# Loading raw second-layer weights into the home of their low part, in a fused attention and two-layer-pair kernel

## The chip, the cores and the metric

The kernel runs on one core of a Trainium2 chip. The metric is the device time of one execution in microseconds, as the median of several runs.

## The reference

Causal attention with a decay term feeds a first pair of dense layers (a softmax-gated activation and a layer norm between them) and then a second pair (squared ReLU between them). What matters here is the last part:

```python
def _moe2_ref(x, w_in, w_out):          # x 2304 x 512, w_in 512 x 2048, w_out 2048 x 512
    h = np.maximum(x @ w_in, 0.0)
    return (h * h @ w_out).astype(np.float32)
...
attn_out = _attn_ref(**attn_kwargs)
x = np.ascontiguousarray(attn_out.transpose(0, 2, 1, 3)).reshape(B * S, H * D)
x = _moe_ref(x=x, **moe_kwargs)
return _moe2_ref(x=x, **moe2_kwargs)
```

All arrays are float32.

## The kernel before

**Precision.** TensorE multiplies numbers in the rounded format fp32r. Each float32 operand is therefore split into a high part (its rounding, made by a copy) and a low part (the operand less its high part, made by a subtraction on VectorE), and each product is three: high x low, low x high, high x high. Line 1139, `halves`, emits the two operations: the rounding by `copy` (line 376 on ScalarE, line 380 on GpSimd, line 382 on VectorE), the subtraction on line 1144.

**Stages.** Attention runs tile by tile, and the first layer pair follows it token block by token block (lines 860 to 862 for its first layer, 811 to 813 for its second). Under both, the second pair's weights are read from the inputs, put together from words of 64-bit numbers, combined for a Strassen scheme and stored to DRAM as w2d, w2u, w2f and w2s; five staging buffers in the tile free serve for that. Then comes the second pair. The first 256 tokens go up in a plain form (`half_up`, line 1334, eight pairs p of feature blocks, products written into z). The other 2048 go up in 32 units of seven Strassen products (`unit`, line 1386). Each pair of each block goes down in a step of seven products (`step`, lines 1487 to 1489, 21 matmuls).

**Weights and homes.** The up weights of the plain form come from w2d, 16 loads of 512 columns (`weightsh`, line 1173). The down weights of seven of the eight pairs come from w2f in four loads each, "a" of 256 columns and "b", "s", "t" of 512 (`weights2`, line 1192); the eighth pair has its split parts stored in w2s and loads them direct (line 1212). Each high or low part lives in a home carved from a tile that an earlier stage used: the attention's k tiles, its pt, the first pair's weights wih, wil, woh, wol, the staging tile free, e and others. `claim` (line 1003) adds a step with no work to the plan that makes a home wait for its last use by the earlier stage.

**The raw ring.** A raw weight is loaded by `load2` (line 1157, transfer on line 1164) into the next of six raw buffers: kn0, kn1, vn4, vn5, x and adj1 (`RAW`, line 1049). `halves` then rounds it from there into the high home and subtracts into the low home; when the subtraction is done, the raw buffer is free. The token blocks of the units use the same six: `xload` (transfer on line 1224), `xdiff` (line 1241), `xsplit` (`halves` into homes in wol, q2 and vn).

**Order.** No engine's order is written by hand. Each operation is a step of a plan, with its engines and costs, a priority (a due time) and what it reads and writes. `lay` (line 127) simulates the five engines with these costs and takes, for each engine, the ready step that starts first, or within a slack the most urgent. A step that falls ready earlier can so pass others on every engine. Raw loads have the priority of their use less AHEAD = 10000 ns; claims had that of the use itself. All transfers are issued by SyncE, one after the other; each holds its waits there.

Of the kernel before, what the change touches and what calls it, by code (L numbers as in the profile page):

```python
# [8 lines left out]
F32 = mybir.dt.float32  # L9
# [4 lines left out]
ALU = mybir.AluOpType  # L14
# [13 lines left out]
class Plan:  # L28
# [11 lines left out]
        dve=dict(pe=230, dve=127, act=198, pool=203, dma=1230),  # L40
        act=dict(pe=110, dve=142, act=153, pool=160, dma=1234),
        pool=dict(pe=135, dve=75, act=75, pool=88, dma=1200),
        dma=dict(pe=1500, dve=1450, act=1410, pool=1450, dma=1790),
# [225 lines left out]
def tile_kernel(ctx: ExitStack, tc: tile.TileContext, q, k, v, f, w_in, w_out, g_ln, w2_in, w2_out, out):  # L269
    nc = tc.nc  # L270
# [31 lines left out]
    w2d = dram.tile([KF2, P, 512], F32, name="w2d")  # L302
    w2u = dram.tile([KF2 // 2, 7, P, 512], F32, name="w2u")
    w2f = dram.tile([KF2 // 2 - NPRE, 7, P, 256], F32, name="w2f")
# [55 lines left out]
    pl = Plan(dict(pp=3, hp=2, rq=NRQ), ("z0", "z1", "xo", "h", "h0", "h1"))  # L360
# [9 lines left out]
    def copy(n, dst, src, prio, reads, writes, uses=(), scale=None, psum=True):  # L370

        def fn():
            x = 1.0 if scale is None else scale
            if s.on == "act":
                if scale is None:
                    nc.scalar.copy(dst(), src())  # L376
                else:
                    nc.scalar.activation(out=dst(), in_=src(), func=AF.Copy, scale=scale)
            elif s.on == "pool":
                nc.gpsimd.tensor_scalar(out=dst(), in0=src(), scalar1=x, scalar2=1.0, op0=ALU.mult, op1=ALU.mult)  # L380
            elif scale is None:
                nc.vector.tensor_copy(dst(), src())
            else:
                nc.vector.tensor_scalar(out=dst(), in0=src(), scalar1=scale, scalar2=None, op0=ALU.mult)

        ap = not (scale is None or isinstance(scale, float))
        ns = dict(act=(51 if psum else 94) + 0.833 * n + (93 if ap else 0))
        ns["dve"] = 67 + 1.042 * n if psum else 68 + 0.522 * n + (61 if ap else 0)
        if not psum:
            ns["pool"] = (244 if ap else 161) + 0.833 * n  # L390
        s = pl.add(ns, fn, prio, reads, writes, uses=uses, port=not psum)
        return s
# [596 lines left out]
    def carve(tag, sizes, dt=F32R, old=None):  # L989

        memo = {}
        out, o = [], 0
        for n in sizes:
            def get(o=o, n=n):
                if "t" not in memo:
                    memo["t"] = new(tag, [sum(sizes)], dt)
                return memo["t"][:, o : o + n]

            out.append((get, held[tag] if old is None else old))
            o += n  # L1000
        return out

    def claim(piece, keys, prio):

        if piece[1]:
            pl.add(dict(dve=0), lambda: None, prio, [], list(piece[1]) + list(keys))

    def rk2(ri):
        return [("2r", ri, z) for z in range(2)]
# [10 lines left out]
    c = carve("woh", [512] * 7 + [256] * 2)  # L1020
# [8 lines left out]
    c = carve("q2", [512] * 4)  # L1029
# [17 lines left out]
    HU = upper[:6] + large[at_h:]  # L1047
    SX2 = carve("adj1", [640], F32, rk2(5))[0]
    RAW = [carve(a, [512], F32)[0] for a in ("kn0", "kn1", "vn4", "vn5", "x", "adj1")]
# [89 lines left out]
    def halves(raw, rk, hi, hk, lo, lk, n, prio, uses=()):  # L1139

        copy(n, hi, raw, prio, rk, [hk], uses, None, False)

        def sub():
            nc.vector.tensor_tensor(out=lo(), in0=raw(), in1=hi().bitcast(F32), op=ALU.subtract)  # L1144

        pl.add(dict(dve=67 + 1.045 * n), sub, prio, list(rk) + [hk], [lk], uses=uses, port=True)
# [3 lines left out]
    def once(nm, piece, keys, prio):  # L1150
        if nm not in first_use:
            first_use.add(nm)
            claim(piece, keys, prio)

    turn = [0]

    def load2(src, rk, n, prio):
        ri = turn[0] % len(RAW)
        turn[0] += 1
        once(("raw", ri), RAW[ri], rk2(ri), prio)  # L1160

        def fn():
            dst = RAW[ri][0]()[:, 0:n]
            nc.sync.dma_start(dst.rearrange("p (c x) -> p c x", x=256) if len(src.shape) == 3 else dst, src)

        pl.add(dict(dma=LOAD2 * n / 512), fn, prio - AHEAD, rk, rk2(ri)[0 : n // 256])
        return ri

    W2 = {p: {} for p in range(KP)}
    H2 = {p: {} for p in range(KP)}  # L1170
    hkeys = {}

    def weightsh(p, prio):
        for c in range(2):
            ri = load2(w2d[2 * p + c], [("w2d", 2 * p + c, z) for z in range(2)], 512, prio)
            for a in "hl":
                m = 4 * p + 2 * c + "hl".index(a)
                hkeys[m] = ("w2", p, f"u{c}{a}")
                H2[p][f"u{c}{a}"] = HU[m]
                claim(HU[m], [hkeys[m]], prio)  # L1180
            W = H2[p]
            halves(
                RAW[ri][0], rk2(ri), W[f"u{c}h"][0], ("w2", p, f"u{c}h"), W[f"u{c}l"][0], ("w2", p, f"u{c}l"), 512, prio
            )

    def again(piece):
        for m, x in enumerate(HU):
            if x is piece:
                return (piece[0], [hkeys[m]])
        return piece  # L1190

    def weights2(p, prio):
        W = W2[p]
        o = 0
        for nm, n in (("a", 256), ("b", 512), ("s", 512), ("t", 512)):
            c = range(o, o + n // 256)
            o += n // 256
            for a in "hl":
                W[nm + a] = again((small if n == 256 else large).pop(0))
                claim(W[nm + a], [("w2", p, nm + a)], prio)  # L1200
            if p < KP - NPRE:
                src = w2f[p, c[0]] if n == 256 else w2f[p, c[0] : c[0] + 2].rearrange("c p x -> p c x")
                ri = load2(src, [("w2f", p, k) for k in c], n, prio)
                halves(
                    lambda ri=ri, n=n: RAW[ri][0]()[:, 0:n], rk2(ri)[0 : n // 256], W[nm + "h"][0], ("w2", p, nm + "h"),
                    W[nm + "l"][0], ("w2", p, nm + "l"), n, prio,
                )
                continue
            for y, a in enumerate("hl"):
                def fn(dst=W[nm + a][0], c=c, n=n, y=y):  # L1210
                    src = w2s[p + NPRE - KP, c[0] : c[0] + n // 256, :, y * 256 : y * 256 + 256]
                    nc.sync.dma_start(
                        dst().bitcast(F32).rearrange("p (c x) -> p c x", x=256), src.rearrange("c p x -> p c x")
                    )

                pl.add(
                    dict(dma=LOAD2 * n / 512), fn, prio - AHEAD, [("w2s", p, k) for k in c], [("w2", p, nm + a)]
                )

    def xload(ri, g, tok, prio):  # L1220
        once(("raw", ri), RAW[ri], rk2(ri), prio)

        def fn():
            nc.sync.dma_start(
                RAW[ri][0]().rearrange("p (c x) -> p c x", x=TB), x2d[:, 2 * g : 2 * g + 2, tok : tok + TB]
            )

        rk = [("x2d", cc, tok // P + t) for t in range(TPB) for cc in (2 * g, 2 * g + 1)]
        pl.add(dict(dma=1140), fn, prio - 2000, rk, rk2(ri))

    def xsplit(ri, j, prio):
        for a in range(2):
            once(("xo", j, a), XOP[j][a], [("xo", j, a)], prio)
        halves(RAW[ri][0], rk2(ri), XOP[j][0][0], ("xo", j, 0), XOP[j][1][0], ("xo", j, 1), 512, prio)
# [10 lines left out]
    def x_half(prio):  # L1245
        for g in range(2):
            xload(g, g, 0, prio)
            xsplit(g, 5 + g, prio)
        turn[0] = 2

    def x_block(b, prio):
        tok = TB + 2 * TB * (b - 1)
# [306 lines left out]
    for y, (a, e) in enumerate(((0, P), (P, S))):  # L1559
        w = slice(a, e)  # L1560
        n = e - a

        def scan(w=w, a=a):
# [8 lines left out]
                out=fl[:, w], in0=fl[:, w], scalar1=1e-4, scalar2=1.0, op0=ALU.max, op1=ALU.min  # L1572
# [91 lines left out]
    t0 = TEND + P2  # L1664
    t1 = t0 + KP * 2800
    x_half(t0 - W2X)
    for x in ORDER:
        nm, p = x[0], int(x[1])
        if nm == "u":
            weightsh(p, t0 - W2H + 2800 * p)  # L1670
        elif nm == "d":
            weights2(p, t1 - W2D + 4830 * p)
        elif nm == "h":
            half_up(p, t0 + 2800 * p)
        else:
            x_block(1, t1 - 9000)
    todo = [(0, p) for p in range(KP)]
    done = 0
    for b in range(1, NTB // 2 + 1):
        for p in range(KP):  # L1680
            n = (b - 1) * KP + p
# [27 lines left out]
AHEAD = 10000.0  # L1709
# [18 lines left out]
NPRE, LOAD2 = 1, 900  # L1728
# [54 lines left out]
```

## Time and profile before

| | |
|---|---|
| runs | 830.59, 824.18 and 828.28 us, median 828.28 |
| the profiled execution | 824.09 us |
| its span in the profile | 822.3 us |
| TensorE busy, mean granted clock | 800.7 us, 0.997 |
| stages, as the trace shows them | attention and first pair to about 468 us; plain up products (L1334) 447 to 483; units and steps from 479 |

Times in the trace count from the start of the span. A row of a timeline gives the start, the duration, the engine, the line, the output and inputs by tile name with numbers left out, and in brackets the idle time before it with what ended it. Matmuls overlap, so a run of n products lasts about n pitches and one tail. "Granted clock" is the share of TensorE's full speed of 2.4 GHz that it was given.

### The profile page before, as it was taken

How to read it: one execution, taken by the hardware profiler on the slowest of the kernel's cores; microseconds unless marked ns; L12 is line 12 of the kernel's file. 1: busy time of each engine (PE TensorE's matmuls, PEld its weight loads, DVE VectorE, ACT ScalarE, POOL GpSimd, SP SyncE). 2: the span in 40 equal slices, each digit the busy share in tenths (PEclk: the TensorE clock that was granted, in tenths of full speed). 3: DMA queues.
4: the chain of work that ended last, by engine and by line, in shares of the span. 5: the costliest groups of instructions: out<-in, count | busy, mean ns of one | idle time of the engine just before them, and what ended most of it. 6: DMA issues, size and time to landing. Idle time of an engine off the chain costs nothing.

```text
span 822.3 us, 19212 instructions
## 1 busy us (share of the span) xinstructions
PE 800.7 (97%) x6648; PEld 734.4 (89%) x6648; DVE 635.1 (77%) x1624; ACT 547.8 (67%) x1409; POOL 390.8 (48%) x539
## 2 busy tenths in 40 slices
PE   8899999999999999999999998999999999999997
PEld 7687777888888888888989998999999999999997
DVE  8898777878886667686658779779778867987776
ACT  6899988888797779899777676445335343533332
POOL 6467776767768777687777411021111121112110
PEclk9999999999999999999999999999999999999999
DMA  6643346657665554765557889896867767665401
GB/s 206 212 142 122 104 116 188 197 153 210 188 182 186 186 188 132 218 202 194 180 201 231 253 270 310 324 317 194 246 206 234 230 192 242 200 224 184 151 14 39
DMA packets 109665, 159.69 MB, mean 194 GB/s; under 512 B 12832, under 2 KB 52768, under 8 KB 109568
## 3 DMA queue, kind: packets, MB, share of 16 engines
q1 hardware_dynamic: 109568, 158.47, 60.5%
q8 instruction: 52, 0.85, 0.5%
q14 instruction: 45, 0.37, 0.2%
HBM read 121.65 MB, written 36.72 MB: 193 GB/s over the span
## 4 chain that ended last, share of the span: by engine, by line
PE 57%; ACT 3%; DVE 3%; issue 2%; DMA 1%; POOL 1%; DVEq 0%; POOLq 0%; ACTq 0%
PE pp L1386 9%; PE z L1386 9%; PE hp L1489 3%; PE hp L1488 3%; PE hp L1487 3%; PE z L1334 3%; PE pp L621 2%; PE z L567 2%; PE pp L811 2%; PE pp L812 2%; PE pp L813 2%; PE xo L641 2%; PE xo L1487 2%; PE xo L1489 2%; PE xo L1488 2%
## 5 line engine op out<-in xcount | busy, mean ns | idle before, releaser
L602 ACT ACTIVATE adj<-z,st 64x288 f32<-64x288 f32 (+9 forms) x192 | 95.1, 499 | 16.9 <-DVE st L588 15.9
L567 PE MATMUL z<-k,q 128*128 128x256 f32 (+17 forms) x384 | 90.0, 332 | 0.9 <-ACT adj L602 0.8
L588 DVE CUSTOM_DVE_ANT_0 z<-z,maskb 128x128 f32<-128x128 f32 (+8 forms) x144 | 65.2, 463 | 29.0 <-PE z L567 26.4
L621 PE MATMUL pp<-ident,adj 128*128 128x128 f32 (+1 forms) x480 | 76.6, 274 | 6.1 <-ACT adj L602 4.9
L812 PE MATMUL pp<-ln,wol 128*128 128x256 f32 x288 | 80.2, 278 | 0.0
L813 PE MATMUL pp<-ln,woh 128*128 128x256 f32 x288 | 80.1, 278 | 0.0
L1144 DVE TENSOR_TENSOR k<-adj,k 128x512 fp32r<-128x512 f32 x75 | 53.0, 706 | 33.8 <-POOL k L380 26.4
L376 ACT COPY pt<-pp 128x256 f32<-128x256 f32 (+5 forms) x169 | 67.2, 418 | 17.2 <-PE pp L621 16.1
L621 PEld LDWEIGHTS pp<-ident,adj 128*128 128x128 f32 (+1 forms) x480 | 50.6, 140 | 30.8 <-ACT adj L602 18.9
L380 POOL TENSOR_SCALAR k<-adj 128x512 fp32r<-128x512 f32 x39 | 24.3, 623 | 89.1 <-PE xo L1489 31.8
L734 POOL TENSOR_TENSOR free<-free 128x256 uint32<-128x256 uint32 x64 | 51.2, 807 | 31.0 <-DVE free L728 24.2
L567 PEld LDWEIGHTS z<-k,q 128*128 128x128 f32 (+3 forms) x384 | 54.9, 177 | 7.5 <-ACT adj L602 3.8
L641 PE MATMUL xo<-pt,vn 128*64 128x128 f32 (+1 forms) x960 | 61.1, 268 | 0.5 <-ACT pt L376 0.3
L860 PE MATMUL hp<-wih,xl 128*128 128x512 f32 x144 | 60.3, 419 | 0.8 <-ACT hp L899 0.8
L641 PEld LDWEIGHTS xo<-pt,vn 128*64 128x64 f32 x960 | 49.0, 137 | 11.3 <-issue 6.3
L861 PE MATMUL hp<-wil,xh 128*128 128x512 f32 x144 | 56.7, 394 | 0.2 <-DVE wil L738 0.2
L862 PE MATMUL hp<-wih,xh 128*128 128x512 f32 x144 | 56.7, 394 | 0.0
L812 PEld LDWEIGHTS pp<-ln,wol 128*128 128x128 f32 x288 | 54.4, 189 | 0.5
L813 PEld LDWEIGHTS pp<-ln,woh 128*128 128x128 f32 x288 | 54.2, 188 | 0.0
L1097 POOL TENSOR_TENSOR free<-free 128x256 f32<-128x256 f32 x64 | 52.5, 820 | 2.9 <-DMA w2f<-free 0.2
L1386 PE MATMUL z<-wol,k 128*128 128x256 f32 x384 | 52.5, 278 | 0.1
L1386 PE MATMUL pp<-wol,ln 128*128 128x256 f32 x384 | 51.9, 278 | 0.0
(597 smaller groups left out, 2686.3 us busy)
## 6 DMA issues: line engine op xcount, KB each, us to landing
k<-w2u SPq DMA_DIRECT2D x96, 256.0 KB
ln<-w2u SPq DMA_DIRECT2D x96, 256.0 KB
w2u<-free SPq DMA_DIRECT2D x56, 256.0 KB
kn<-in_k_dram SPq DMA_DIRECT2D x32, 256.0 KB
free<-in_moe_w_out_dram SPq DMA_DIRECT2D x32, 256.0 KB
free<-in_moe_w_in_dram SPq DMA_DIRECT2D x32, 256.0 KB
q<-w2u SPq DMA_DIRECT2D x32, 256.0 KB
w2f<-free SPq DMA_DIRECT2D x49, 128.0 KB
```

Source lines behind the costliest of these rows:

```text
L376: nc.scalar.copy(dst(), src())
L567: nc.tensor.matmul(dst, lhsT=ql[0:r, p, 0:m], rhs=rhs, start=(g == 0), stop=(g == 1))
L588: nc.vector.tensor_tensor_reduce(out=z, in0=z, in1=maskb[0:m, o : o + e - a], scale=1.0, scalar=st[0:m, 0:1] if y else 3e38, op0=ALU.add, ...
L602: nc.scalar.activation(out=adj[0:m, c[1] : c[2]], in_=Z[c[0]][0:m, 0 : c[2] - c[1]], func=AF.Exp, bias=st[0:m, low : low + 1], scale=-1.0, ...
L621: nc.tensor.transpose(at(sk)[:, (c - g) * m : (c - g + 1) * m], adj[0:m, zc : zc + P], ident[0:m, 0:m])
L641: nc.tensor.matmul(XO[own[j], g // 2, off : off + m], lhsT=VN[vslot[b, c]][:, (g + j) * D : (g + j + 1) * D], rhs=PT[(s - h + g + j) % NPT ...
L812: nc.tensor.matmul(px, lhsT=wol[:, fc, w], rhs=hi, start=False, stop=False)
L813: nc.tensor.matmul(px, lhsT=woh[:, fc, w], rhs=hi, start=False, stop=(fc == KF - 1))
L860: nc.tensor.matmul(HP[:, c], lhsT=XL[i][:, cc, :], rhs=wih[:, cc, w], start=(cc == 0), stop=False)
L861: nc.tensor.matmul(HP[:, c], lhsT=XH[i][:, cc, :], rhs=wil[:, cc, w], start=False, stop=False)
L862: nc.tensor.matmul(HP[:, c], lhsT=XH[i][:, cc, :], rhs=wih[:, cc, w], start=False, stop=(cc == KC - 1))
L1386: nc.tensor.matmul(half(i), lhsT=l, rhs=r[:, c * TB : c * TB + TB], start=(j == start), stop=(j == 5), skip_group_check=True,)
```

## The change

`load2` goes, and `within` takes its place for weights. The transfer writes the raw weight into the home of the low part; the rounding reads it there and writes the high home; the subtraction reads low and high home and writes the low home in place. Both claims are made due AHEAD earlier, with the load. The token blocks keep the six buffers, and the ring's turn counter goes.

```diff
-    def load2(src, rk, n, prio):
-        ri = turn[0] % len(RAW)
-        turn[0] += 1
-        once(("raw", ri), RAW[ri], rk2(ri), prio)
+    def within(src, rk, hi, hk, lo, lk, n, prio):
 
         def fn():
-            dst = RAW[ri][0]()[:, 0:n]
+            dst = lo().bitcast(F32)
             nc.sync.dma_start(dst.rearrange("p (c x) -> p c x", x=256) if len(src.shape) == 3 else dst, src)
 
-        pl.add(dict(dma=LOAD2 * n / 512), fn, prio - AHEAD, rk, rk2(ri)[0 : n // 256])
-        return ri
+        pl.add(dict(dma=LOAD2 * n / 512), fn, prio - AHEAD, rk, [lk])
+        copy(n, hi, lambda: lo().bitcast(F32), prio, [lk], [hk], (), None, False)
+
+        def sub():
+            nc.vector.tensor_tensor(out=lo(), in0=lo().bitcast(F32), in1=hi().bitcast(F32), op=ALU.subtract)
+
+        pl.add(dict(dve=67 + 1.045 * n), sub, prio, [hk], [lk], port=True)
...
-                claim(HU[m], [hkeys[m]], prio)
+                claim(HU[m], [hkeys[m]], prio - AHEAD)
...
-                claim(W[nm + a], [("w2", p, nm + a)], prio)
+                claim(W[nm + a], [("w2", p, nm + a)], prio - AHEAD)
...
-        turn[0] = 2
```

The plan comes out otherwise. Line numbers after the change are four to six lower in `weightsh` and `weights2` and two lower behind them (L1384 for L1386, L1485 to L1487 for L1487 to L1489, L1223 for L1224).

First SyncE, at the end of the first pair. Before, from the last up load (kn<-w2d) on; vn, kn and x are raw buffers, k and ln homes of the units' weights:

```order
L1164 DMA kn_50_4662<-w2d 128x512
L1224 DMA vn_50_5380<-x2d 128x2x256
L1375 DMA k_50_5408<-w2u 128x512
L1224 DMA vn_50_5425<-x2d 128x2x256
L1375 DMA k_50_5408<-w2u 128x512
L1224 DMA kn_50_4662<-x2d 128x2x256
L1375 DMA k_50_5408<-w2u 128x512
L1375 DMA k_50_5323<-w2u 128x512
L1375 DMA ln_50_6046<-w2u 128x512 x4
L1164 DMA kn_50_4662<-w2f 128x256
L1164 DMA kn_50_4740<-w2f 128x2x256
```

After, from the first load into woh on; woh, free, wil and k are now the destinations of raw loads:

```order
L1159 DMA woh_5907<-w2f 128x256
L1159 DMA free_5929<-w2f 128x2x256 x2
L837 DMA x2d<-xc_1416 128x256
L1159 DMA free_5929<-w2f 128x2x256
L1159 DMA woh_5907<-w2f 128x2x256 x4
L1373 DMA k_50_5304<-w2u 128x512
L1159 DMA wil_5545<-w2f 128x2x256 x3
L1373 DMA q_50_5365<-w2u 128x512
L1373 DMA ln_50_6086<-w2u 128x512 x3
L1159 DMA k_50_5206<-w2f 128x2x256 x2
L1159 DMA k_50_5318<-w2f 128x2x256
L1373 DMA ln_50_6086<-w2u 128x512 x3
```

The weight loads stand together and ahead of the units' own loads; the four x2d loads of the first token block, three of them among the rows of before, have moved some twenty rows up. Behind the rows of after follow, up to the loads for the third unit: xc (128 columns halved), two k, one pt from w2f, one q and three k from w2u.

Second TensorE, at the step of pair 2 whose second part begins with xo<-woh (L1487 before, L1485 after). Before:

```order
L1386 MATMUL pp_125<-wol_5996,ln_50_6046 128x256 x12
L1386 MATMUL pp_127<-wol_5996,ln_50_6046 128x256 x6
L1487 MATMUL xo<-woh_5855,k_50_5323 128x256
L1488 MATMUL xo<-woh_5855,k_50_5323 128x256
L1489 MATMUL xo<-woh_5855,k_50_5323 128x256
```

After:

```order
L1487 MATMUL hp<-free_5929,ln1a_5937 128x256
L1485 MATMUL xo<-woh_5907,k_50_5304 128x256
L1486 MATMUL xo<-woh_5907,k_50_5304 128x256
L1487 MATMUL xo<-woh_5907,k_50_5304 128x256
L1485 MATMUL pp_126<-free_5929,k_50_5304 128x256
```

Before, the step is cut, with two units' products between its parts; after, its two parts are one run. Counted in matmuls from the last L1334 (L1332 after) on, the order after is: unit 12, down 9, unit 30 with 12 down between, unit 24, down 9, unit 6, down 12, unit 12, then pair 2's step, 9 and 12 (126 matmuls stand ahead of it), then the third unit's first 24. The last block of L811 to L813 has 96 L1334 products ahead of it, where it had 78, and 96 behind it.

Third VectorE, the splits before that same step. Before, with the low part of the step's activations as the last row (k<-adj,k, the releaser of the step):

```order
L1144 TENSOR_TENSOR wil_5512<-vn_50_5425,wil_5512 128x512
L1412 TENSOR_TENSOR maskb_6172<-maskb_6172,pp_127 128x256
L1412 TENSOR_TENSOR ln1b_6082<-xw_6123,z_122 128x256 x2
L1144 TENSOR_TENSOR wil_5512<-adj_50_5282,wil_5512 128x512
L1144 TENSOR_TENSOR wil_5512<-kn_50_4662,wil_5512 128x512
L1412 TENSOR_TENSOR xl_50_5609<-maskb_6172,pp_125 128x256
L1412 TENSOR_TENSOR xl_50_5609<-xl_50_5609,pp_125 128x256
L1144 TENSOR_TENSOR wil_5512<-kn_50_4740,wil_5512 128x512
L1144 TENSOR_TENSOR k_50_5323<-adj_50_5620,k_50_5323 128x512
```

After, from the token block's two splits into vn on:

```order
L1144 TENSOR_TENSOR vn_50_5403<-adj_50_5749,vn_50_5363 128x512
L1144 TENSOR_TENSOR vn_50_5367<-vn_50_5685,vn_50_4776 128x512
L1165 TENSOR_TENSOR woh_5907<-woh_5907 128x512
L1410 TENSOR_TENSOR xw_6082<-xw_6082,z_121 128x256
L1165 TENSOR_TENSOR woh_5907<-woh_5907 128x512
L1165 TENSOR_TENSOR wil_5545<-wil_5545 128x512
L1410 TENSOR_TENSOR ln1b_6070<-xw_6082,z_122 128x256
L1410 TENSOR_TENSOR ln1b_6070<-ln1b_6070,z_122 128x256
L1165 TENSOR_TENSOR wil_5545<-wil_5545 128x512 x2
L1144 TENSOR_TENSOR ln1a_5937<-adj_50_5729,ln1a_5937 128x384
L1144 TENSOR_TENSOR k_50_5304<-adj_50_5665,k_50_5304 128x512
```

The low part of the step's activations still stands behind wil splits; their inputs now come from their own homes, and the vn splits have moved ahead of the first unit's additions (L1410).

## Rows read from the trace of the kernel before

**Rows 1.** The page's head: span, and busy time of each engine.
```profile
span 822.3 us, 19212 instructions
PE 800.7 (97%) x6648; PEld 734.4 (89%) x6648; DVE 635.1 (77%) x1624; ACT 547.8 (67%) x1409; POOL 390.8 (48%) x539
```

**Rows 2.** Stages: length, then PE, PEld, DVE, ACT, POOL busy, PEclk, DMA share, GB/s.
```profile
480.00:500.00 20.00, 17.18 (x144) 16.69 (x143) 16.06 (x31) 15.20 (x32) 1.38 (x2) 1.00 0.86 275
500.00:520.00 20.00, 19.71 (x150) 19.14 (x150) 17.28 (x46) 10.01 (x21) 2.09 (x2) 0.91 1.01 341
...
600.00:650.00 50.00, 50.00 (x438) 50.00 (x437) 42.12 (x108) 21.90 (x46) 8.46 (x15) 1.00 0.68 218
```

**Rows 3.** TensorE's waits, 400 to 822 us: total, times, longest.
```profile
PE xo L1487 <- DVE k L1144: 3.0, 2, 2.8
PE pp L1487 <- DVE k L1144: 0.7, 1, 0.7
```

**Rows 4.** Timeline of TensorE around the gap.
```profile
494.45 2.28 PE L1386 MATMUL pp<-wol,ln 128*128 128x256 f32 x18
499.48 0.38 PE L1487 MATMUL xo<-woh,k 128*128 128x256 f32 x1 [2.75 <-DVE k L1144]
...
505.45 0.38 PE L1487 MATMUL xo<-wil,k 128*128 128x256 f32 x1 [0.29 <-DVE k L1144]
```

**Rows 5.** Stretches of 4 us, TensorE alone: busy, granted clock, DMA share, GB/s.
```profile
500.00:504.00 4.00, 4.00 (x23) 0.58 0.90 290
...
516.00:520.00 4.00, 4.00 (x36) 1.00 1.05 387
...
536.00:540.00 4.00, 4.00 (x38) 1.00 0.99 299
```

**Rows 6.** The chain that ended last, 491 to 500 us: start, length, what.
```profile
491.79 0.68 DVE woh L1144
492.50 4.83 DMA kn<-w2f
497.48 0.63 POOL wil L380
498.13 0.30 DVE wil L1144
...
498.74 0.70 DVE k L1144
499.48 0.38 PE xo L1487
```

**Rows 7.** Timeline of SyncE: transfers at their issue.
```profile
480.01 0.36 SPq L1224 DMA_DIRECT2D kn<-x2d  x1
...
481.40 1.94 SPq L1375 DMA_DIRECT2D ln<-w2u  x4
486.66 0.97 SPq L1164 DMA_DIRECT2D kn<-w2f  x2
...
491.16 1.70 SPq L1164 DMA_DIRECT2D kn<-w2f  x2
...
497.72 1.50 SPq L1164 DMA_DIRECT2D kn<-w2f  x2
```

**Rows 8.** SyncE's waits, 440 to 525 us.
```profile
SPq L1164 <- DVE q L1144: 3.9, 2, 2.7
SPq L1164 <- DVE k L1144: 3.8, 4, 1.8
SPq L1164 <- DVE wil L1144: 3.5, 4, 1.2
SPq L1164 <- DVE pt L1144: 2.8, 2, 1.4
```

**Rows 9.** Timeline of VectorE: the token block's first difference.
```profile
484.01 0.69 DVE L1241 TENSOR_TENSOR x<-kn,kn 128x512 f32<-128x512 f32 x1 [2.38 <-DMA kn<-x2d]
```

**Rows 10.** Timelines of VectorE and ScalarE: subtractions in place and not, a rounding.
```profile
463.97 0.28 DVE L1457 TENSOR_TENSOR adj<-adj,xh 128x128 f32<-128x128 f32 x1
464.17 0.28 DVE L1457 TENSOR_TENSOR adj<-adj 128x128 f32<-128x128 f32 x1
...
469.02 0.41 DVE L1144 TENSOR_TENSOR woh<-kn,free 128x256 fp32r<-128x256 f32 x1
469.36 0.68 DVE L1144 TENSOR_TENSOR free<-x,free 128x512 fp32r<-128x512 f32 x1
...
495.25 0.62 ACT L376 CAST wil<-kn 128x512 fp32r<-128x512 f32 x1
```

**Rows 11.** Timeline of TensorE: end of the first pair, plain up products.
```profile
468.11 0.28 PE L813 MATMUL pp<-ln,woh 128*128 128x256 f32 x1
...
469.64 6.64 PE L1334 MATMUL z<-vn,k 128*128 128x256 f32 x54
```

**Rows 12.** TensorE's waits, 0 to 440 us.
```profile
PE pp L621 <- ACT adj L602: 4.9, 10, 1.3
```

More of the change, by code (lines that the diff above doesn't have):

```diff
@@ L1153, in once @@
             claim(piece, keys, prio)
-    turn = [0]
-    def load2(src, rk, n, prio):
-        ri = turn[0] % len(RAW)
-        turn[0] += 1
-        once(("raw", ri), RAW[ri], rk2(ri), prio)
+    def within(src, rk, hi, hk, lo, lk, n, prio):
         def fn():
-            dst = RAW[ri][0]()[:, 0:n]
+            dst = lo().bitcast(F32)
             nc.sync.dma_start(dst.rearrange("p (c x) -> p c x", x=256) if len(src.shape) == 3 else dst, src)
-        pl.add(dict(dma=LOAD2 * n / 512), fn, prio - AHEAD, rk, rk2(ri)[0 : n // 256])
-        return ri
+        pl.add(dict(dma=LOAD2 * n / 512), fn, prio - AHEAD, rk, [lk])
[3 more added lines that the diff above has]
+        pl.add(dict(dve=67 + 1.045 * n), sub, prio, [hk], [lk], port=True)
     W2 = {p: {} for p in range(KP)}
@@ L1174, in weightsh @@
         for c in range(2):
-            ri = load2(w2d[2 * p + c], [("w2d", 2 * p + c, z) for z in range(2)], 512, prio)
             for a in "hl":
@@ L1179, in weightsh @@
                 H2[p][f"u{c}{a}"] = HU[m]
-                claim(HU[m], [hkeys[m]], prio)
+                claim(HU[m], [hkeys[m]], prio - AHEAD)
             W = H2[p]
-            halves(
-                RAW[ri][0], rk2(ri), W[f"u{c}h"][0], ("w2", p, f"u{c}h"), W[f"u{c}l"][0], ("w2", p, f"u{c}l"), 512, prio
+            within(
+                w2d[2 * p + c], [("w2d", 2 * p + c, z) for z in range(2)],
+                W[f"u{c}h"][0], ("w2", p, f"u{c}h"), W[f"u{c}l"][0], ("w2", p, f"u{c}l"), 512, prio
             )
@@ L1199, in weights2 @@
                 W[nm + a] = again((small if n == 256 else large).pop(0))
-                claim(W[nm + a], [("w2", p, nm + a)], prio)
+                claim(W[nm + a], [("w2", p, nm + a)], prio - AHEAD)
             if p < KP - NPRE:
                 src = w2f[p, c[0]] if n == 256 else w2f[p, c[0] : c[0] + 2].rearrange("c p x -> p c x")
-                ri = load2(src, [("w2f", p, k) for k in c], n, prio)
-                halves(
-                    lambda ri=ri, n=n: RAW[ri][0]()[:, 0:n], rk2(ri)[0 : n // 256], W[nm + "h"][0], ("w2", p, nm + "h"),
+                within(
+                    src, [("w2f", p, k) for k in c], W[nm + "h"][0], ("w2", p, nm + "h"),
                     W[nm + "l"][0], ("w2", p, nm + "l"), n, prio,
```

## The prediction

> **What bounds the kernel now.** The page comes first: TensorE is busy for 97% of the span and VectorE for 77% [rows 1]. So the most that a change outside TensorE can return is what TensorE loses: idle time, and time at the lower clock. The stages show where that lies. From 600 us on TensorE is busy for 50.00 of 50.00 us; the stretch from 480 to 520 us, where the kernel passes from the first layer pair to the second, is the only late one with both losses: 17.18 of 20 us busy in its first half and a mean granted clock of 0.91 in its second [rows 2]. After 400 us TensorE's named waits are 3.0 us at L1487 and 0.7 us at the same line with another bank, both for the splitting line L1144 on VectorE [rows 3].
>
> The timeline puts the big one in its place. TensorE ends 18 products of an "up" unit (L1386) at 494.45 + 2.28 = 496.73 us, and the next instruction, L1487 of the "down" step for pair 2, starts at 499.48: 2.75 us idle. A second gap of 0.29 us stands at 505.45 [rows 4]. After the big gap the granted clock falls: 0.58 over 500 to 504 us, that is mostly the 1.2 GHz level instead of 2.4, and 23 products in 4 us where 36 to 38 are usual [rows 5]. The cost is 4 x (1 - 0.58) = 1.68 us.
>
> The chain of waits says who made the gap [rows 6]. Read backward: L1487 waits for a low part on VectorE (498.74, 0.70 us); that stands in VectorE's queue behind the splitting of weights for pair 4 (tile wil, 498.13), which waited for its rounding on GpSimd (497.48), which waited 4.83 us for a transfer kn<-w2f begun at 492.50. kn is one of the six raw buffers. SyncE shows why the transfer was late: for the six raw buffers the loads come in turns, 486.66, 491.16 and 497.72 for the two named kn [rows 7], and SyncE's waits name L1164 (the raw load) waiting for L1144 (the subtraction that frees a raw buffer): 3.9, 3.8, 3.5, 2.8 us and more [rows 8]. And at 484.01 VectorE stood still 2.38 us for kn<-x2d [rows 9]: the next token block needs the same raw buffers and had been queued behind weights.
>
> **The change part by part.** 44 raw loads pass through the ring now: 16 for the up weights (8 pairs x 2) and 28 for the down weights (7 pairs x 4).
>
> *Counts.* Nothing is added or removed: 44 transfers of the same bytes, 44 roundings (0.62 us on ScalarE for 512 columns, [rows 10]) and 44 subtractions (0.68 us, same group). Only the source becomes the destination. Subtraction in place is in the trace already: adj<-adj took 0.28 us at 464.17, and adj<-adj,xh, with one input elsewhere, 0.28 us at 463.97 [rows 10]. Cost 0; bounds -1 to +1 us in all, from reading 44 x 0.02 us of scatter as real.
>
> *The ring's stall.* A raw load now waits for its own home to be free, not for one of six buffers. The order shows what this frees. The four x2d loads go out long before the last first-layer product, so the first up unit stands right behind the last half-block product (L1334) instead of behind pair 2's first down products; and the loads for pairs 2 to 6 follow one another on SyncE without waiting for a subtraction. I work out whether they come in time. The last reading of woh is the last L813, at 468.11 us, and 18 L1334 products now stand ahead of that block. L1334 runs at (6.64 - 0.28) / 53 = 0.12 us [rows 11], so woh is free at 468.3 + 2.1 = 470.4. From there SyncE issues, behind the wait for woh, 29.5 loads of 256 KB (halves counted as half) up to the three for the third up unit: 29.5 x 0.262 = 7.7 MB. At 387 GB/s, the best stretch of the trace, that takes 20 us, at 275 GB/s, the mean of 480 to 500 [rows 2, 5], 28 us: they land at 490.4 to 498.4. TensorE wants them after 96 L1334 products (to 481.8 us) and 147 products more, at (2.28 - 0.28) / 17 = 0.118 each [rows 4], so at 499.1. The margin is 0.7 to 8.7 us. Pair 2's S products, which wait now, come at about 481.8 + 135 x 0.118 = 497.7; their four woh loads are among the first nine, landed by 480, and split on VectorE before 490. So the 2.75 us and the 0.29 us go, and with the gap its low clock: 2.75 + 0.29 + 1.68 = 4.7 us. What is late next is the third up unit's load, by the smaller margin.
>
> *A wait added.* A transfer into woh, free, pt, e or k now waits on SyncE for the last reader of that home, and what is queued behind it waits too: at woh that is a store of x2d, the down weights of pairs 2 to 6 and the up weights of units 1 and 2, for which TensorE waits in the end. I take 0, since the loads above come in time from 470.4 on; the upper bound is rival (b). That SyncE stands at such waits is in the trace: 3.9 us for one group of raw loads, up to 2.7 us at once [rows 8]. The Trainium skill (DMA: Bandwidth & Descriptors, "Anatomy of one DMA — SWDGE (gpsimd) path") has the rule that speaks against the change here: the DMA engines never wait on semaphores, the issuing sequencer does, before it dispatches. The trace agrees with it, the raw loads leaving only when SyncE's wait ends. Under that rule one late home delays all 29.5 loads and (b) is possible; if each transfer waited by itself, (b) would fall away and the sum would stay at 4.7.
>
> *VectorE's queue.* The two X splits into the vn tiles now stand in front of unit 0's additions, and wait for the last L1334 at 481.8. VectorE is held until about 482.5; its first customer behind that, the addition for unit 0, is wanted only after 12 more products. Cost 0; bounds 0 to 1.5 us (two subtractions and a rounding).
>
> *Early loads.* Four 128 KB loads move into attention (small homes fall free there). Each costs a SyncE issue of some 0.4 us, a rounding and a subtraction of 0.41 us. TensorE there waits for ScalarE's exponentials in ten places, 4.9 us in all, 1.3 at most [rows 12]. Bounds 0 to 4 x 0.8 = 3.2 us, if each of the four fell ahead of such an exponential; I take 0, as four short pieces among some 400 us of attention seldom do.
>
> Sum: 4.7 us. The profiled execution took 824.09 us (span 822.3 and 1.8 around it), so 819.4 on its footing. The three runs have the median 828.28, 4.2 us above it, so 823.6.
>
> **The rivals.** (a) *The gap only moves*: VectorE is busy for 16.06 of 20 us in 480 to 500 and 17.28 in the next 20 [rows 2], and the transfers run near their best. If splitting or transfer is the limit of this passage and the ring only shows it, another step waits as long, with the low clock after it: 828.3. For it: 1.01 of the DMA share in 500 to 520. Against: the chain runs through a load that began late, and VectorE was idle ahead of it.
>
> (b) *SyncE is held too long*, the slower side. The place is the woh wait; the price is a microsecond on TensorE for each microsecond of release past the margin. It decides from about 471 us at 275 GB/s and from 479 us at 387. Released at 480, where the last x2d load and the ln loads leave today [rows 7], the third unit's loads land at 480 + 28 = 508, 8.9 us late, and with a low-clock stretch of 1.7 the loss is 10.6, less the 4.7 won: +5.9, 834.2. Against: L813 ends by its own products, not by the new queue.
>
> (c) *More is won*: products run at 36 per 4 us in 516 to 520 and 38 in 536 to 540 [rows 5]. If the crowding of transfers slows them for the 20 us from 508 to 528, another 20 x 2 / 38 = 1.1 us goes: 822.5.
>
> (d) *It doesn't bite*: the ring costs nothing net, as units only swap places with down steps: 828.3, with (a) in time.
>
> **How the numbers follow.** Forecast 0.50, (a) and (d) together 0.25, (b) 0.15, (c) 0.10. The forecast's own range is 819 to 828, from the bounds above and from runs of before that lie 6.4 us apart. The low end takes (c) and the lowest run of before (824.18 - 5.8 = 818.4) with some room: 816; the high end takes (a), (d) and the nearer half of (b): 832. A measurement of this kernel can tell about 1%, or 8.3 us, from no change. Forecast, (a), (c) and (d) lie inside it: 0.78. Faster by more would need nearly all of TensorE's idle time back: 0.12. Slower by more is (b) with a later release: 0.10.
>
> **What would show it.** Right: no L1487 wait above 0.5 us between 480 and 520, granted clock 1.00 throughout, first L1386 next to the last L1334 at about 482, raw loads leaving SyncE back to back after 470. Wrong: TensorE idle for over 2 us at another line there, with the loads landing after 499; or SyncE standing at a home while the attention stage loses time.

## The result, and the profile after

The changed kernel takes 818.54 us (median of 6 runs, 817.78 to 819.82); the kernel before took 825.53 us beside it (6 runs, 823.82 to 830.59). The ratio is 0.9907, with a 95% interval of 0.9878 to 0.9937: 7.0 us less by the medians. The two profiled executions, 824.09 us before and 817.78 us after, are 6.3 us apart.

The head of the page after, to be held against [rows 1]:

```profile
span 816.0 us, 19207 instructions
PE 798.1 (98%) x6648; PEld 732.3 (90%) x6648; DVE 635.6 (78%) x1624; ACT 545.6 (67%) x1407; POOL 393.3 (48%) x541
```

VectorE does the same work in the same time (635.6 against 635.1 us) and the span is 6.3 us shorter. The stages of [rows 2] after:

```profile
480.00:500.00 20.00, 20.00 (x177) 20.00 (x176) 17.82 (x35) 13.15 (x27) 5.44 (x7) 1.00 1.08 364
500.00:520.00 20.00, 20.00 (x179) 20.00 (x178) 15.37 (x44) 7.91 (x17) 2.34 (x4) 1.00 0.90 303
...
600.00:650.00 50.00, 50.00 (x438) 50.00 (x437) 42.87 (x112) 22.38 (x46) 7.72 (x13) 1.00 0.73 232
```

The 40 us of the passage now hold 177 + 179 products where they held 144 + 150, at a granted clock of 1.00. The stage at 600 us has the same 438 as before. TensorE's waits from 400 us to the end, against [rows 3]:

```profile
PE pp L1485 <- DVE k L1144: 0.7, 1, 0.7
```

Only the wait near 798 us is left, which was there before. TensorE's timeline, against [rows 4]: the last product that reads woh, the first product of a unit, pair 2's S step, and the third unit.

```profile
470.33 0.28 PE L813 MATMUL pp<-ln,woh 128*128 128x256 f32 x1
...
481.94 0.28 PE L1384 MATMUL z<-wol,k 128*128 128x256 f32 x1
...
497.32 0.28 PE L1485 MATMUL xo<-woh,k 128*128 128x256 f32 x1
...
498.68 0.28 PE L1384 MATMUL z<-wol,k 128*128 128x256 f32 x1
```

VectorE's timeline shows the step's low part, VectorE's last row in the chain of [rows 6], where it stood at 498.74:

```profile
485.11 0.68 DVE L1165 TENSOR_TENSOR wil<-wil 128x512 fp32r<-128x512 f32 x1
...
488.62 0.87 DVE L1144 TENSOR_TENSOR k<-adj,k 128x512 fp32r<-128x512 f32 x1
```

It is done at 489.49, 7.8 us before TensorE wants it. The first of the two rows is a subtraction in place: 0.68 us, as with another input in [rows 10]. SyncE's timeline, against [rows 7]:

```profile
470.63 0.32 SPq L1159 DMA_DIRECT2D woh<-w2f  x1
471.12 0.88 SPq L1159 DMA_DIRECT2D free<-w2f  x2
...
473.03 2.08 SPq L1159 DMA_DIRECT2D woh<-w2f  x4
...
475.72 1.49 SPq L1159 DMA_DIRECT2D wil<-w2f  x3
```

The loads for pairs 2 to 6 begin as the last reader of woh ends (470.33 + 0.28 = 470.61), and from there to the last row shown SyncE pauses for no more than 0.2 us between two transfers. And three of the 4-us stretches, against [rows 5]:

```profile
488.00:492.00 4.00, 4.00 (x38) 1.00 1.08 361
...
500.00:504.00 4.00, 4.00 (x38) 1.00 1.04 386
...
524.00:528.00 4.00, 4.00 (x36) 1.00 0.02 5
```

**Where the time came from.** I matched the n-th product's start in the trace after with the n-th before, from 442 us on. The difference, by the time before, stays within 0.2 us of zero until 486 us; it is 0.2 us at 490, 3.6 at 500, 6.2 at 510, 7.0 at 531 and 6.3 from 545 to the end. So the whole net gain is made in the passage, and all but 0.1 us of it by 510.

### The profile page after: what moved, and what is told of

Same layout as the page of the kernel before. It is cut to its first block, busy times and chain, and to the rows that moved or that the text cites. A ratio compares the mean times of both kernels' runs of the same rounds, so it can differ in the third digit from the quotient of the medians.

```text
span 816.0 us, 19207 instructions
## 1 busy us (share of the span) xinstructions
PE 798.1 (98%) x6648; PEld 732.3 (90%) x6648; DVE 635.6 (78%) x1624; ACT 545.6 (67%) x1407; POOL 393.3 (48%) x541
## 4 chain that ended last, share of the span: by engine, by line
PE 59%; DVE 3%; ACT 3%; issue 1%; POOL 1%; DMA 1%; DVEq 0%; POOLq 0%; ACTq 0%; SPq 0%
PE z L1384 9%; PE pp L1384 9%; PE hp L1485 3%; PE hp L1486 3%; PE hp L1487 3%; PE z L1332 3%; PE pp L621 2%; PE z L567 2%; PE pp L811 2%; PE pp L812 2%; PE pp L813 2%; PE xo L641 2%; PE xo L1486 2%; PE xo L1487 2%; PE hp L860 2%; PE xo L1485 2%
## 5 line engine op out<-in xcount | busy, mean ns | idle before, releaser
L1144 DVE TENSOR_TENSOR k<-adj,k 128x512 fp32r<-128x512 f32 x72 | 50.9, 707 | 38.4 <-POOL k L380 30.6
L813 PE MATMUL pp<-ln,woh 128*128 128x256 f32 x288 | 80.0, 278 | 0.0
L813 PEld LDWEIGHTS pp<-ln,woh 128*128 128x128 f32 x288 | 54.1, 188 | 0.0
L1384 PE MATMUL z<-wol,k 128*128 128x256 f32 x384 | 52.4, 276 | 0.0
L1089 POOL TENSOR_TENSOR free<-free 128x256 fp32r<-128x256 f32 x63 | 48.4, 784 | 7.3 <-ACT free L376 5.0
```

The costliest lines, as they stand in the source:

```text
L813: nc.tensor.matmul(px, lhsT=woh[:, fc, w], rhs=hi, start=False, stop=(fc == KF - 1))
L1384: nc.tensor.matmul(half(i), lhsT=l, rhs=r[:, c * TB : c * TB + TB], start=(j == start), stop=(j == 5), skip_group_check=True,)
```

## The experiments

A median mixes the passage with attention, whose order the plan also shuffles. So the table sets beside each median the second layer pair alone: from the start of the first plain up product to the start of the last product of all, both read from TensorE's timeline of the profiled execution, one for each kernel.

| kernel | median us | ratio to before, 95% | first up product | last product | between | against before |
|---|---|---|---|---|---|---|
| before | 825.53 | | 447.34 | 817.32 | 369.98 | |
| after | 818.54 | 0.9907 (0.9878, 0.9937) | 447.39 | 811.02 | 363.63 | -6.35 |
| e1_up_only | 823.68 | 0.9983 (0.9956, 1.0009) | 448.25 | 816.90 | 368.65 | -1.33 |
| e2_down_only | 819.89 | 0.9941 (0.9921, 0.9961) | 448.60 | 813.09 | 364.49 | -5.49 |
| e3_late_claims | 819.12 | 0.9927 (0.9899, 0.9954) | 453.10 | 815.76 | 362.66 | -7.32 |
| e5_early_claims | 825.24 | 0.9990 (0.9971, 1.0009) | 448.43 | 818.38 | 369.95 | -0.03 |
| e4_ring_in_plan | 823.57 | 0.9970 (0.9945, 0.9996) | 449.08 | 817.12 | 368.04 | -1.94 |
| e7_ring12_in_plan | 824.17 | 0.9977 (0.9952, 1.0002) | 449.17 | 817.24 | 368.07 | -1.91 |
| e9_six_apart | 822.54 | 0.9969 (0.9952, 0.9987) | 449.25 | 816.76 | 367.51 | -2.47 |
| e10_down_six_apart | 819.94 | 0.9933 (0.9916, 0.9950) | 448.74 | 812.85 | 364.11 | -5.87 |
| e8_ahead16 | 820.29 | 0.9942 (0.9926, 0.9958) | 448.98 | 813.12 | 364.14 | -5.84 |
| e6_hold1 | 821.23 | 0.9952 (0.9936, 0.9969) | 447.68 | 813.57 | 365.89 | -4.09 |
| e6_hold3 | 830.55 | 1.0059 (1.0031, 1.0087) | 448.41 | 822.65 | 374.24 | +4.26 |
| e6_hold6 | 838.44 | 1.0143 (1.0105, 1.0182) | 448.02 | 831.34 | 383.32 | +13.34 |

The theory: the six buffers, shared by token block and down weights, make the gap. The rivals: the up loads do it, or the earlier claims alone do.

**Which loads: e1_up_only and e2_down_only.** Each makes the change for one kind of load and keeps the ring for the other.

```diff
 # e1: in weights2 (down weights); e2: the same in weightsh (up weights)
-                within(
+                ringed(
```

`ringed` is the old `load2` with `halves` behind it; the claims of the ringed kind stay at `prio`.

> Only the 16 up loads go into the home of their low part; the 28 down loads pass through the six raw buffers as before. Theory (the wait for a raw buffer in front of pairs 2 to 6 made the gap): the down loads still wait, so most of the loss stays, 823 to 826 us, with a TensorE wait of 1 us or more between 480 and 520. Rival (the gain comes from the up loads leaving the ring early, so that the token block's loads get their buffers): 818 to 820.

> Only the 28 down loads go into their homes; the 16 up loads pass through the six raw buffers. Theory: the down loads were what waited, so most of the gain is there, 818 to 821 us and no gap above 0.5 us between 480 and 520. Rival (the up loads matter): 823 to 826.

With the down loads ringed the steps still wait, in smaller pieces; TensorE's timeline of e1:

```profile
505.06 0.39 PE L1504 MATMUL xo<-wil,k 128*128 128x256 f32 x1 [0.51 <-DVE k L1144]
...
509.15 0.38 PE L1504 MATMUL hp<-q,ln1a 128*128 128x256 f32 x1 [1.64 <-DVE ln1a L1144]
510.94 0.39 PE L1504 MATMUL xo<-wil,k 128*128 128x256 f32 x1 [0.46 <-DVE k L1144]
```

Matched with the changed kernel, e1 is 1.1 us behind at 458 already, where a product of L938 has waited 0.86 us for GpSimd; the rest of its 5.0 us comes behind 499. Without the down loads in the ring (e2), no wait is above 0.43 us between 480 and 520, and 5.49 of the 6.35 us come. The down loads carry the change; the up loads are small.

**The claims: e3_late_claims and e5_early_claims.** e3 is the changed kernel with the claims due as before; e5 is the kernel before with only the claims due earlier.

```diff
 # e5; e3 is the reverse, in the changed kernel
-                claim(HU[m], [hkeys[m]], prio)
+                claim(HU[m], [hkeys[m]], prio - AHEAD)
...
-                claim(W[nm + a], [("w2", p, nm + a)], prio)
+                claim(W[nm + a], [("w2", p, nm + a)], prio - AHEAD)
```

> All 44 loads in place as in the changed kernel, but the claims of the homes are due with the use, as before the change, not 10000 ns earlier. Theory (place, not due time): 818 to 820 us. Rival (the earlier claims alone moved the order): 823 to 826.

> The kernel before with the ring kept, its claims made due 10000 ns earlier. Theory: the ring still holds the loads, 824 to 827 us, gap kept. Rival (earlier claims): 818 to 820.

e3 loses nothing that can be measured, e5 wins nothing. TensorE's timeline of e5 still has its gap:

```profile
501.59 0.58 PE L1487 MATMUL hp<-ws,ln1a 128*128 128x256 f32 x1 [3.75 <-DVE ln1a L1144]
```

That rival falls. (e3's profiled execution ran part of attention at a lower clock, which is why its first up product stands at 453.10.)

**Wait or order: e4_ring_in_plan.** The ring can hurt in two ways: a transfer waits on SyncE for a buffer, or the plan, which knows the buffers, lays another order. e4 loads in place, so no transfer waits for a raw buffer, but the plan still counts six turns.

```diff
+        ri = turn[0] % len(RAW)
+        turn[0] += 1
+        once(("raw", ri), RAW[ri], rk2(ri), prio)
+        rr = rk2(ri)[0 : n // 256]
...
-        pl.add(dict(dma=LOAD2 * n / 512), fn, prio - AHEAD, rk, [lk])
+        pl.add(dict(dma=LOAD2 * n / 512), fn, prio - AHEAD, rk, [lk] + rr)
...
-        pl.add(dict(dve=67 + 1.045 * n), sub, prio, [hk], [lk], port=True)
+        pl.add(dict(dve=67 + 1.045 * n), sub, prio, [hk] + rr, [lk], port=True)
```

> The loads go into their own homes as in the changed kernel, so no transfer waits for a raw buffer; but the plan still counts six turns of a ring and orders the work as if they were waited for. It separates the wait itself from the order that the plan makes of it. Theory A (the wait at a raw buffer on SyncE made the loss): with the wait gone the time stays near the changed kernel, 818 to 821 us, even in a ring's order, with no TensorE wait above 0.5 us between 440 and 545 us. Theory B (the order that the ring forces on units and down steps is what loses time, since a low part asked for early stands behind splits of weights in VectorE's queue): a gap of 1 to 4 us stays and the granted clock falls behind it, 823 to 829 us. The order counted in matmuls puts down steps between short pieces of units here, and VectorE's splits for pair 3 right ahead of its low part, so I give B somewhat more than half.

Theory A falls: with no weight load waiting at a raw buffer only 1.94 of the 6.35 us come back. B holds in its time, but not in its clock: the idle time lies in pieces of 1.12 us and less, and the granted clock stays at 1.00 behind each. TensorE's timeline of e4:

```profile
492.04 0.97 PE L1391 MATMUL pp<-wol,ln 128*128 128x256 f32 x6 [1.12 <-DVE wol L1144]
...
496.50 0.98 PE L1391 MATMUL z<-wol,k 128*128 128x256 f32 x6 [0.64 <-DVE xw L1417]
...
515.46 0.39 PE L1492 MATMUL xo<-pt,k 128*128 128x256 f32 x1 [0.84 <-DVE k L1144]
```

So the order that the plan makes around the ring is enough for most of the loss. What the wait alone would cost in the new order couldn't be tried: a load into a reused buffer has to stand behind the subtraction that frees it, and the changed kernel has issued eleven raw loads from 470.63 to 477.2 us, with three of their subtractions done by then, so six buffers don't hold it.

**Too few, or shared: e7_ring12_in_plan, e9_six_apart, e10_down_six_apart.** e7 gives the plan twelve turns, six of them still the token block's buffers. e9 gives it six that the token block doesn't use. e10 is e9 with the up weights free of turns.

```diff
 # e7, against e4
-        ri = turn[0] % len(RAW)
+        ri = turn[0] % 12
...
 # e9, against e4
-        once(("raw", ri), RAW[ri], rk2(ri), prio)
-        rr = rk2(ri)[0 : n // 256]
+        rr = [("turn", ri, z) for z in range(n // 256)]
...
 # e10, against e9: turns only where lk[2][0] != "u"
```

> As the run before it with six turns kept in the plan (823.6 us, TensorE idle for 1.1, 0.8, 0.6 and 0.3 us between 488 and 526 us, the granted clock at 1.00), but with twelve turns: the transfers still go into their own homes and wait for no raw buffer. If the ring's cost is the order that the plan has to make around six turns, twelve loosen that order and most of those waits go: 818 to 821 us, with less than 1 us of named TensorE waits between 440 and 545. If those waits came from something else in that kernel than the ring's turns (a lower priority of the down loads, say), they stay: 823 to 824.

> As the run with six turns kept in the plan (823.6 us), but the six turns are the weights' own: the token block's loads and differences take none of them. Twelve turns, six of them the token block's buffers, had left the time at 824.2. If the loss comes from the token block sharing its buffers with the weights (its loads then stand behind the down weights, the units start later and the down steps come before their activations' low parts are split), six turns apart give 818 to 820.5 us with the x2d loads ahead of the first load into woh and under 0.8 us of named TensorE waits between 440 and 545. If the number of turns is the limit, it stays at 822.5 to 825 with waits of 1 us and more.

> As the run with six turns of the weights' own (822.5 us), but only the down weights count turns; the up weights load freely. That run had no wait at a down step between 482 and 545 us, but TensorE idle for 1.59 and 0.34 us at 478 to 480.5 for an up weight (tile pt) whose load left SyncE at 473.90, behind the first load into woh, and the granted clock at 0.50 to 0.85 behind it. If that is all that six own turns cost, the load of pt leaves before 460 here, those waits go and the time is that of the changed kernel: 818 to 820 us, the clock at 1.00. If six turns are too few for the down weights, waits of 0.5 us and more show between 482 and 545 and the time stays above 821.

Twelve turns changed nothing, against what I expected. TensorE's timeline of e7:

```profile
502.68 0.39 PE L1493 MATMUL hp<-ws,ln1a 128*128 128x256 f32 x1 [1.56 <-DVE ln1a L1144]
...
513.75 0.39 PE L1493 MATMUL xo<-k,k 128*128 128x256 f32 x1 [1.25 <-DVE k L1144]
```

In e7 the last of the block's four x2d loads leaves SyncE at 477.30, after the first load into woh; in e9 it leaves at 461.39. SyncE's timelines of e7 and e9:

```profile
477.30 0.47 SPq L1230 DMA_DIRECT2D kn<-x2d  x1
```

```profile
461.39 0.46 SPq L1228 DMA_DIRECT2D vn<-x2d  x1
```

No wait at a step is left in e9 between 482 and 545. e9 loses its time elsewhere, and its rows show how. TensorE first, then the chain of waits read forward:

```profile
479.78 0.39 PE L1337 MATMUL z<-vn,pt 128*128 128x256 f32 x1 [1.59 <-POOL pt L380]
480.51 4.52 PE L1337 MATMUL z<-vn,pt 128*128 128x256 f32 x23 [0.34 <-DVE pt L1170]
```

```profile
473.90 5.14 DMA pt<-w2d
479.04 0.07 issue
479.11 0.63 POOL pt L380
479.76 0.70 DVE pt L1170
480.51 1.60 PE z L1337 x9
```

An up load, which takes turns with the down weights here, has slipped behind SyncE's wait for woh. Matched with the changed kernel, e9 has lost 3.9 us by 485, and the same 3.9 us at the end. Freed of turns (e10), the up loads leave before 458.6, as SyncE's timeline of e10 shows, the wait goes, and the passage is 0.5 us from the changed kernel's:

```profile
458.24 0.32 SPq L1165 DMA_DIRECT2D e<-w2d  x1
```

So six turns are enough for the down weights; what cost time was that the token block and the up weights took turns among them.

SyncE's timelines of all the kernels without a hold bear this out. Two times sort them: when the last of the first block's four x2d loads leaves, and when the last up load (from w2d) does. Both leave at 473.8 to 480.3 in the kernel before, e5, e4 and e7, and none of these wins over 1.94 us. In e1 only the x2d loads are late (478.06, the last up load 456.67), and it wins 1.33; in e9 only the up loads (476.49, the last x2d load 461.39), and it wins 2.47. In the changed kernel and in e2, e3, e8 and e10 both have left by 465.3, and these win 5.49 to 7.32. For e9 the chain above runs through the late load; for the others it is shown only that late loads and loss go together. Loads in place with turns shared by the token block and the down weights alone were not run; e1, the nearest, has them share the real ring.

**Earlier still: e8_ahead16.** An attempt to beat the changed kernel.

```diff
-AHEAD = 10000.0
+AHEAD = 16000.0
```

> The changed kernel with its weight loads and claims due 16000 ns ahead instead of 10000. TensorE of the changed kernel has no wait left in the down steps but 0.7 us near the end, so nothing is to be won by still earlier loads: 817.5 to 819.5. The claim that the loads' lead decides how fast this passage runs would want 1 us and more: under 817.5. Earlier claims could also hold SyncE longer at homes in attention: 819.5 to 822.

The passage gains nothing (364.14 us), and the time is that of the third expected case: attention loses 1.6 us, the first up product starting at 448.98. TensorE's waits in e8, 0 to 440 us, against the ten places and 4.9 us of [rows 12] and the ten places and 4.5 us in the changed kernel:

```profile
PE pp L621 <- ACT adj L602: 10.0, 18, 1.2
```

TensorE stands longer for ScalarE's exponentials. Two more things differ there. The granted clock is 0.75 from 15 to 20 us and 0.57 from 20 to 25, where the changed kernel has 1.00. And the trace holds 206 instead of 256 of the products that the plan puts into TensorE's idle stretches (L1694), so part of the longer waits is time that was filled before. Whether SyncE, held at a home, brings this about wasn't separated from the new order.

**A late home: e6_hold1, e6_hold3, e6_hold6.** Rival (b) by itself. A chain of 1 + N transfers within DRAM, each waiting for the one before, holds SyncE right ahead of the first load into woh. Nobody reads what it writes; the output is computed in full.

```diff
...
+            if lk == ("w2", 0, "al"):
+                nc.sync.dma_start(hold[0], w2s[0, 0])
+                for i in range(HOLD_N):
+                    nc.sync.dma_start(hold[i + 1], hold[i])
             dst = lo().bitcast(F32)
```

> The changed kernel with SyncE held on purpose right ahead of the first raw load into woh: a chain of 1 + 3 transfers of 256 KB within DRAM, each waiting for the one before, whose result nobody reads. If one such transfer takes 2 us, as the loads of this stretch do, SyncE is held some 6 to 8 us and the first load into woh leaves at 476 to 479 instead of 470.6. Theory (SyncE's queue is in order and the loads have a margin of a few us, as rival (b) of the prediction had it): by the prediction's margin of 0.7 to 8.7 us this lies at the edge: 818 to 822 us, and if TensorE waits, it waits at the third unit or at a product with woh, for 0 to 4 us. Rival (every transfer only waits for its own data, so the hold delays nobody): 818.5 with the load into woh still at 470.6. Rival (no margin at all): 818.5 + 7 + 1.7 of low clock = 827.

> The same with 1 + 6 transfers: SyncE held 12 to 16 us, first load into woh at 483 to 487. Theory: past the margin by 4 to 12 us, each of them a microsecond of TensorE, and then a stretch at the lower clock worth 1.7 us: 818.5 + 6 to 14 = 824 to 832 us, likeliest 828, with a named TensorE wait of 4 us and more between 490 and 515, and a granted clock below 0.8 in the 4 us behind it. Rival (the hold delays nobody): 818.5. Rival (the lower clock in the kernel before came from something else than the idle time): the same wait, with the granted clock at 1.00 behind it.

> The changed kernel with SyncE held by a chain of 1 + 1 transfers ahead of the first load into woh. With 3 and 6 in the chain that load left at 480.0 and 488.4, and TensorE waited 7.25 and 16.16 us, at a plain up product, for ScalarE, in whose queue a rounding of the late weight stood ahead. That is 1 us for each us beyond a margin of 1.2 to 1.6 us (9.4 and 17.8 us late, less 1.0 and 0.6 us by which TensorE itself came later there). Here the load should leave at about 474.1, 3.5 us late: TensorE idle for 1.5 to 2.3 us at the same product. If the granted clock falls only behind a longer stop, the time is that and some tenths more, 820 to 821.5; if it falls behind this one too, 821.5 to 823.5. If the margin is the one of the prediction (the third unit), no wait and 818.5.

The first two came out slower than expected: a transfer of the chain took 2.8 to 3.5 us and not 2, and the margin was smaller than mine and at another place. SyncE's timeline of e6_hold3:

```profile
470.52 0.58 SPq L1161 DMA_DIRECT2D hold<-w2s  x1
473.55 6.36 SPq L1163 DMA_DIRECT2D hold<-hold  x3
480.00 0.53 SPq L1165 DMA_DIRECT2D woh<-w2f  x1
```

ScalarE's timeline of the same kernel, and then TensorE's:

```profile
483.03 0.40 ACT L378 CAST free<-woh 128x256 fp32r<-128x256 f32 x1 [8.78 <-DMA woh<-w2f]
483.34 0.58 ACT L1304 ACTIVATE z<-z 128x512 f32<-128x512 f32 x1
483.95 0.60 ACT L1309 ACTIVATE q<-z 128x512 f32<-128x512 f32 x1
```

```profile
471.45 5.90 PE L1338 MATMUL z<-vn,k 128*128 128x256 f32 x48
484.60 5.69 PE L1338 MATMUL z<-vn,pt 128*128 128x256 f32 x30 [7.25 <-ACT q L1309]
```

The rounding of the late weight stands in ScalarE's queue ahead of the activations that free the bank z for TensorE's next plain up products. No unit is involved. With the load 3.0, 9.4 and 17.8 us late (473.65, 480.00 and 488.41 against 470.63), of which TensorE itself came 0.3, 1.0 and 0.6 us later to these products, it stood idle for 1.42, 7.25 and 16.16 us: a microsecond for each microsecond beyond a margin of 1.0 to 1.3 us. The changed kernel's own timelines give nearly that margin, ScalarE first and then TensorE:

```profile
474.14 0.60 ACT L1303 ACTIVATE q<-z 128x512 f32<-128x512 f32 x1
```

```profile
470.44 5.90 PE L1332 MATMUL z<-vn,k 128*128 128x256 f32 x48
476.18 3.76 PE L1332 MATMUL z<-vn,pt 128*128 128x256 f32 x30
```

ScalarE is done with the second activation at 474.74, 1.4 us before TensorE goes on. TensorE in e6_hold1, for what follows:

```profile
478.04 4.11 PE L1338 MATMUL z<-vn,pt 128*128 128x256 f32 x30 [1.42 <-ACT q L1309]
```

## Why the prediction was right

**The mechanism held, row by row.** The forecast put the last reader of woh at 470.4 (470.33 + 0.28 in the trace), the first unit at 481.8 (481.94), pair 2's S products at 497.7 (497.32) and the third unit at 499.1 (498.68). No L1485 wait stands in 480 to 520, the clock is 1.00, and the loads leave back to back. The edits that I costed at nothing cost nothing: VectorE's busy time rose by 0.5 us in all, the subtraction takes the same 0.68 us, the first up product starts 0.05 us later, so attention lost nothing to the four early loads. That the token block's x2d loads shared the buffers, which the prediction read from [rows 9], is by e9 and e10 one part of the matter; the up loads' turns are another. What I didn't see is that the ring acts through the plan's order: in e4 no weight load waits at a raw buffer, and it still loses 4.4 of the 6.35 us.

**The size.** Predicted were 823.6 us; 818.54 came, inside the range. The range, 816 to 832 us, also holds "no change" at 828.3, so it is the rows above and not the time that tell the forecast from (a) and (d). Of the 5.1 us between them, 2.75 are the footing (828.28 from three runs, 825.53 from six) and 2.3 the sum: 4.7 forecast, 7.0 by the medians, 6.35 between the products of the profiles. Both made the forecast too slow, so neither hid the other. The step that was mis-sized is "2.75 + 0.29 + 1.68 = 4.7 us". Its three terms, measured between the starts of products, are 2.91 (from 496.45 to 499.48, less one product of 0.118), 0.45 (from 504.88 to 505.45, less one) and 1.53 (the 17 products that start from 500.64 on take 3.53 us to 504.17, instead of 17 x 0.118): 4.9. So the terms were sound, and what lacked was a fourth of about 1.5 us. About half of it is late starts: between 483 and 545 us ten products start 0.16 to 0.35 us behind the one ahead of them, too soon to stand among the waits, and after the change three do. The other half is spacing: the other products there start 0.1164 us apart before and 0.1148 after. e6_hold1 shows late starts without a gap of the ring's: with 1.42 us idle and the clock at 1.00 the passage is 2.26 us longer, 0.35 of it in the 30 products behind the stop, which take 4.11 us where the changed kernel's take 3.76. What sets the spacing stays open.

**The rivals.** (a) and (d), no net gain, fall with the ratio. (c) foresaw more in the right amount (822.5 from the same 828.28, so -5.8) for a wrong reason: 38 products run in 4 us at a DMA share of 1.08 and 36 at 0.02, so crowding by transfers doesn't slow them. (b) didn't happen, as woh came free when its products ended, but its mechanism is real. For a release at 480 it had +5.9 us against before; e6_hold3, with the load leaving at 480.00, measured +4.7 (830.55 against 825.88). The price of 1 us for each us was right; the place was not. I had the third unit and a margin of 0.7 to 8.7 us there; it is ScalarE's queue at the plain up products, with 1.0 to 1.4 us. The Trainium skill (DMA: Bandwidth & Descriptors, "Anatomy of one DMA — SWDGE (gpsimd) path") has the rule that the issuing sequencer waits and not the DMA engine. The three runs agree with it for SyncE's transfers: the load into woh, whose home was free by 471.7, left at 473.65, 480.00 and 488.41, behind the hold. The up load of e9 that left at 473.90, behind the load into woh at 471.05, fits it too. One remark of the prediction doesn't follow from its rows: a gain of over 8.3 us wouldn't take nearly all of TensorE's idle time, which is 822.3 - 800.7 = 21.6 us in [rows 1]; only a chance rested on it.

## What to carry to other kernels

Where two streams with different due times take turns in the same buffers, look at the sharing before the number: twelve turns, six of them shared, won nothing over six shared (1.91 against 1.94 us), and six that the down weights had for themselves won nearly all that unlimited homes did (5.87 of 6.35). A planner that knows the buffers builds their limits into every engine's order, so the loss may stand as waits for VectorE, with no wait at a buffer left to see. And when a load is moved earlier into a home that it must wait for, ask which engine's queue its first consumer stands in: here that engine's next work, and not the load's user, set the margin.

## What the runs showed of the hardware

TensorE's clock didn't follow the length of a stop alone. Behind 2.75 us [rows 4, 5], 3.75, 7.25 and 16.16 us idle it was at 1.2 GHz for some us; behind 1.56 and 1.25 us in e7, 1.42 us in e6_hold1 and 1.64 us in e1 (with 0.46 us more 1.3 us later) it stayed at 2.4 GHz. But in e9, idle for 1.59 us and 0.34 us with one product between, it fell; its stretches of 2 us (TensorE alone, columns as in [rows 5]):

```profile
478.00:480.00 2.00, 0.41 (x3) 1.00 0.99 322
480.00:482.00 2.00, 1.66 (x11) 0.85 1.05 379
482.00:484.00 2.00, 2.00 (x11) 0.50 1.09 383
```

What makes the difference between e1 and e9 isn't shown. And the transfers ran at a DMA share of 1.08 and 364 GB/s from 480 to 500 us without any loss to TensorE, which was busy for 20.00 of the 20 us with 177 products.
